# Five columns of a row vector on 128 partitions: turned on chip by DVE and PE instead of gathered from DRAM

## The chip, the cores and the metric

One of the eight cores of a Trainium2 chip runs the whole program. The metric is the time of one execution in device microseconds (us). A profiled execution adds a trace: each instruction of the engines PE (matrix products), PEld (their weight loads), DVE (vector), ACT (scalar functions), POOL and SP (which here only issues DMAs), and each packet that the 16 DMA engines moved.

## What is computed

One token with D = 1024 goes through a layernorm and then through two branches whose results are added to it.

```python
xn = _layernorm(x, axis=-1)
return x + _A_ref(xn, A_k_cache, A_v_cache, A_wq, A_wo) + _B_ref(xn, B_w1, B_w2, B_w3, B_w4)
```

Branch A is attention of 32 query heads on 4 key heads with a cache of 65536 keys of 128 numbers each, in bf16. Branch B mixes through w1 and w2, and adds a feed-forward part; only this part is touched here:

```python
x1 = x + hs
h2 = _gelu(_layernorm(x1, axis=-1) @ w3) @ w4
```

As Sq is 1, the shifted mix is taken apart in the kernel so that w3 needs only the normed token. `h = gelu(xn2 @ w3)` has F = 3584 numbers, and w4 has 3584 rows of 1024.

## The kernel before, in words

**Weights and cache are streamed.** 170 MB come from DRAM through three SBUF slots of 64 KB on each of 128 partitions (`big`, line 71). The list `slots` (lines 117 to 128) sets the order: wq; then for each of the 4 key heads two K pieces and two V pieces in turn (K0, V0, K1, V1 and so on; 8 MB each, and each worked off in two halves of 16384 keys); w3 stands between V0 and K1; w1, the first piece of w4 and the "x4" rows stand after the third head; wo, w2 and the rest of w4 come last. The loop at lines 548 to 555 works off slot i after it has issued slot i + 2 (`ensure`, line 193), and `issue` (line 160) puts one DMA in SP's queue. SP takes its DMAs strictly in this order, and each waits until the slot that it overwrites has been read by its last instruction. So V1 waits for V0's last product, and K2, the next in SP's queue, waits behind V1.

**K** (`compute_K`, line 426): DVE transposes the 8 MB in place, 4 instructions for each half (line 435); PE forms scores (line 439); DVE, PE and ACT form the maximum, the exponential and its transpose `pT` (lines 443 to 476). **V** (`compute_V`, line 479): 32 products add into `oacc`, one PSUM tile with one buffer (line 482). The first half of a head is copied to `og` by ACT (line 491), and each other half is added by DVE (line 494). A half's products wait until `oacc` has been read.

**w3** (`compute_w3`, line 375): 64 products (line 322) give h in rows: h lies on partitions 0, 32, 64 and 96, in two banks of 448 columns each. ACT applies gelu into `hrow` (line 379).

**The bounce** (`bounce`, line 360): w4 needs h on partitions, so POOL writes h to a DRAM scratch `scr_h` (line 363) and reads 3200 of its numbers back as `dst_h`, 25 columns on 128 partitions (line 367). The remaining 384 rows of w4 are the x4 rows: gathered by two indirect DMAs from lines 164 to 171, 70 partitions with 4 rows each and 104 partitions with 1 row each, as the table `XP` (line 24) says. The matching 384 numbers of h are gathered from `scr_h` into columns 25 to 29 of `dst_h` by two more indirect DMAs (lines 369 to 372, issued at line 156): 8 bytes on each of 70 partitions, then 2 bytes on each of 104. A partition without a row has an index out of bounds and keeps the zero that a memset of POOL put there (line 366). The columns are used at line 424, some 190 us later.

**Order of instructions.** The text above gives only the order in which the program is written. A scheduler orders each engine's instructions when the program is built, and pools decide about buffers: `pT` has two (line 76), `pm` in PSUM two (line 80).

Of the kernel before, what the change touches and what calls it, by code (L numbers as in the profile page):

```python
# [8 lines left out]
BF16 = mybir.dt.bfloat16  # L9
F32 = mybir.dt.float32  # L10
# [13 lines left out]
XR = (4, 1)  # L24
XP = (((0, 15), (16, 20), (28, 44), (48, 52), (60, 70), (72, 74), (76, 78), (80, 82), (84, 87), (92, 100), (124, 128)),
      ((0, 20), (28, 52), (60, 88), (92, 120), (124, 128)))
# [5 lines left out]
def kernel(  # L32
# [14 lines left out]
    nc = tc.nc  # L47
    P = 128
# [7 lines left out]
    F = B_w3.shape[1]  # L56
    DC = D // P
    FC = F // P
    NOUT = A_wo.shape[1]
# [4 lines left out]
    FW = F // 8  # L64
# [7 lines left out]
    const = ctx.enter_context(tc.tile_pool(name="const", bufs=1))  # L72
# [3 lines left out]
    tpool = ctx.enter_context(tc.tile_pool(name="tp", bufs=2))  # L76
# [3 lines left out]
    ps_M = ctx.enter_context(tc.tile_pool(name="psM", bufs=2, space=bass.MemoryType.PSUM))  # L80
# [5 lines left out]
    FB = sum(W4_PIECES)  # L86
    w4_v = B_w4[0:P * FB, :].rearrange("(m c) n -> m c n", c=FB)
    x_n = [sum(b - a for a, b in r) for r in XP]
    x_start = [P * FB + sum(XR[j] * x_n[j] for j in range(i)) for i in range(len(XR) + 1)]
    assert x_start[-1] == F and all(x_start[i] % r == 0 and F % r == 0 for i, r in enumerate(XR))  # L90
    wo_v = A_wo.rearrange("(p j) n -> p (j n)", p=P)
    w1_v = B_w1.rearrange("(p c) n -> p (c n)", c=DC)
    w2_v = B_w2.rearrange("(m c) n -> m (c n)", c=DC)
# [4 lines left out]
    def source(piece):  # L98
        kind = piece[0]
        if kind == "wq":  # L100
            return wq_v
        if kind == "w3":
            return w3_v
        if kind == "w1":
            return w1_v
        if kind == "w2":
            return w2_v
        if kind == "wo":
            return wo_v
        if kind == "w4":  # L110
            c0 = w4_start[piece[1]]
            return w4_v[:, c0:c0 + W4_PIECES[piece[1]], :].rearrange("p c n -> p (c n)")
        _, g, t, _ = piece
        cache = A_k_cache if kind == "K" else A_v_cache
        return cache[0, g, t * BK:(t + 1) * BK, :].rearrange("(p k) d -> p (k d)", p=P)
# [14 lines left out]
    st = {}  # L130
# [3 lines left out]
    x_row = []  # L134
# [17 lines left out]
                end = b  # L152
            nc.vector.tensor_copy(out=x_row[i][:], in_=row)

    def gather_rows(i, dst, src):
        nc.gpsimd.indirect_dma_start(out=dst, out_offset=None, in_=src,
                                     in_offset=bass.IndirectOffsetOnAxis(ap=x_row[i][:, 0:1], axis=0),
                                     bounds_check=x_start[i + 1] // XR[i] - 1, oob_is_err=False)

    def issue(pieces):  # L160
        t = big.tile([P, SLOT], BF16, name="slot")
        at = 0
        for piece in pieces:
            if piece[0] == "x4":
                w = sum(XR) * NOUT
                loaded[piece] = t[:, at:at + w]
                nc.gpsimd.memset(loaded[piece], 0.0)  # L167
                for i, r in enumerate(XR):
                    gather_rows(i, t[:, at:at + r * NOUT], B_w4.rearrange("(u r) n -> u (r n)", r=r))
                    at += r * NOUT  # L170
                continue
            src = source(piece)
            w = src.shape[-1]
            nc.sync.dma_start(out=t[:, at:at + w], in_=src)
            loaded[piece] = t[:, at:at + w]
            if piece[0] in ("K", "V"):
                for h in range(HALVES):
                    loaded[(piece[0], piece[1], HALVES * piece[2] + h)] = t[:, h * KEYS:(h + 1) * KEYS]
            at += w
        assert at <= SLOT  # L180
# [3 lines left out]
    for a in range(4):  # L184
        nc.scalar.dma_start(out=x_bf[32 * a:32 * a + 32, :],  # L185
                            in_=A_x[0, 0, 32 * a * DC:(32 * a + 32) * DC].rearrange("(p c) -> p c", c=DC))
# [6 lines left out]
    def ensure(upto):  # L193
        while n_issued[0] <= min(upto, len(slots) - 1):
            issue(slots[n_issued[0]])
            n_issued[0] += 1
# [5 lines left out]
    ident_bf = early[:, 0:64].bitcast(BF16)  # L202
# [68 lines left out]
    for j in range(4):  # L271
# [22 lines left out]
                          in_=sel8[:].unsqueeze(2).to_broadcast([P, 8, 4]))  # L294
# [10 lines left out]
    for b in range(2):  # L305
        for par in range(2):
            nc.vector.tensor_copy(out=psel[:, 2 * b + par, :].rearrange("p (a i) -> p a i", a=4),
                                  in_=iv[:, b, par, :].unsqueeze(1).to_broadcast([P, 4, 32]))


    def rows_product(key, part, wt, xp, width, n_chunks):
        if part == 0:
            st[key] = ps_S.tile([P, 2, 512], F32, name="rows", tag="sc")
        acc = st[key]
        n_c = wt.shape[1]
        for cl in range(n_c):
            c = n_c * part + cl
            for j in range(4):
                for bk in range(2):
                    ch = 4 * bk + j  # L320
                    if ch < n_chunks:
                        nc.tensor.matmul(acc[32 * j:32 * j + 32, bk, 0:width], lhsT=xp[:, c, :],  # L322
                                         rhs=wt[:, cl, ch * width:(ch + 1) * width],
                                         start=(c == 0), stop=(c == DC - 1), tile_position=(0, 32 * j),
                                         skip_group_check=True)
        return acc
# [30 lines left out]
                             skip_group_check=True)  # L357
        nc.vector.tensor_copy(out=qsel[:], in_=pq[:])

    def bounce(rows_ap, view, n, C, tag, extra=False):  # L360
        scr = dram.tile([1, n], BF16, name=f"scr_{tag}")
        flat = scr[0, :]
        nc.gpsimd.dma_start(out=view(flat), in_=rows_ap)
        dst = const.tile([P, C + (sum(XR) if extra else 0)], BF16, name=f"dst_{tag}")
        if extra:
            nc.gpsimd.memset(dst[:, C:], 0.0)
        nc.gpsimd.dma_start(out=dst[:, 0:C], in_=flat[0:P * C].rearrange("(p c) -> p c", c=C))
        if extra:
            at = C
            for i, r in enumerate(XR):  # L370
                gather_rows(i, dst[:, at:at + r], flat.rearrange("(u r) -> u r", r=r))
                at += r
        return dst

    def compute_w3():
        wt = loaded[("w3",)].rearrange("p (c n) -> p c n", n=F)
        acc = rows_product("psh", 0, wt, xpad2, FW, 8)
        hrow = ppool.tile([P, 2, FW], BF16, name="hrow", tag="p")
        nc.scalar.activation(out=hrow[:], in_=acc[:, :, 0:FW], func=ACTF.Gelu_apprx_tanh)
        st["hT"] = bounce(hrow[:].rearrange("(j u) b n -> j u b n", u=32)[:, 0],  # L380
                          lambda f: f.rearrange("(b j n) -> j b n", b=2, j=4), F, FB, "h", True)

    def compute_w1():
        wt = loaded[("w1",)].rearrange("p (c n) -> p c n", n=D)
        acc = rows_product("psh1", 0, wt, xpad2, 512, 2)
        h1row = ppool.tile([64, 512], BF16, name="h1row", tag="p")
        nc.scalar.activation(out=h1row[:], in_=acc[0:64, 0, :], func=ACTF.Gelu_apprx_tanh)
        grow = tpool.tile([64, 512], BF16, name="grow", tag="pT")
        nc.vector.memset(grow[:], 0.0)
        cq = D // 4  # L390
        for grp, shift in enumerate((1, -1, 2, -2)):
            for s in range(S):
                if 0 <= s - shift < S:
                    r0, c0 = 32 * (grp // 2), cq * (grp % 2)
                    nc.vector.tensor_copy(out=grow[r0:r0 + 1, c0:c0 + cq], in_=h1row[r0:r0 + 1, c0:c0 + cq])
        st["gT"] = bounce(grow[:].rearrange("(j u) n -> j u n", u=32)[:, 0],
                          lambda f: f.rearrange("(j n) -> j n", j=2), D, DC, "g")
# [142 lines left out]
    def compute_wo():  # L540
        wt = loaded[("wo",)].rearrange("p (j n) -> p j n", n=NOUT)
        pair_open(wt.shape[1] + DC)
        for j in range(wt.shape[1]):
            pair_acc(oT[:, j:j + 1], wt[:, j, :])

    compute = {"wq": compute_wq, "w3": compute_w3, "w1": compute_w1, "w2": compute_w2, "w4": compute_w4, "x4": compute_x4,
               "wo": compute_wo, "K": compute_K, "V": compute_V}
    for i, pieces in enumerate(slots):
# [37 lines left out]
```

## Time and profile before

| what | value |
|---|---|
| time, median of 3 runs | 403.15 us (402.7 to 404.05) |
| the profiled execution's own time | 402.7 us |
| its span in the profile | 400.9 us |
| mean granted TensorE clock | 0.816 |
| busy: PE, DVE, ACT, POOL | 215.5, 220.8, 35.7, 14.7 us |
| DMA packets and bytes | 4236, 170.11 MB |
| bytes read by the queue of SP's DMAs | 169.09 MB |
| bytes through the queue of POOL's DMAs | 0.81 MB |

Three views matter here. The page divides the span into 40 slices of 10.0 us, with the mean busy share of the 16 DMA engines and what they moved in GB/s in each. The timeline lists instructions by their start, with their length, engine, source line, what they write and read, and in brackets the idle time before them with what ended it. The trace's packet records give start, length and size of each DMA packet. The engines that moved them are not named, but a packet starts within some 10 ns of the end of the one before on its engine, so each engine can be followed from packet to packet.

### The profile page before, as it was taken

What the parts mean: (1) busy time and instruction counts of PE and PEld (TensorE: products, weight loads), DVE (VectorE), ACT (ScalarE), POOL (GpSimd) and SP (SyncE); (2) the same over time, 40 slices, a digit from 0 to 9 for tenths busy, and PEclk for the clock granted to TensorE, in tenths of its full rate; (3) what the DMA queues carried; (4) which work ended last, traced back from release to release, by engine and by line L of the source; (5) the groups of instructions that cost most, each with busy time, mean ns of one, the idle gap of its engine ahead of it and who ended that gap; (6) DMA issues with size and microseconds to landing.
All of it is one profiled execution on the core that took longest, in us unless ns stands there. A gap on an engine that the chain in (4) does not pass through costs nothing.

```text
span 400.9 us, 3470 instructions
## 1 busy us (share of the span) xinstructions
PE 215.5 (54%) x1450; PEld 87.9 (22%) x1450; DVE 220.8 (55%) x319; ACT 35.7 (9%) x62; POOL 14.7 (4%) x24
## 2 busy tenths in 40 slices
PE   0004778630885197409674953395800965295663
PEld 0002223210332032103221321142400422041321
DVE  0007599401986498429846972597503973497300
ACT  0001000500012001100110011001300021001100
POOL 3000000002000000000000004100000000000000
PEclk9999969875698689957955999589865898599757
DMA  9999999999999999999999999999999999999995
GB/s 386 451 419 419 418 420 452 463 427 426 373 446 432 432 426 414 451 432 451 420 438 418 427 458 432 423 427 410 471 419 418 445 438 459 432 419 418 420 416 226
DMA packets 4236, 170.11 MB, mean 424 GB/s; under 512 B 887, under 2 KB 899, under 8 KB 1207
## 3 DMA queue, kind: packets, MB, share of 16 engines
q1 hardware_dynamic: 3608, 169.09, 97.8%
q0 software_dynamic: 416, 0.81, 0.5%
q8 instruction: 11, 0.18, 0.2%
q10 hardware_dynamic: 196, 0.00, 0.0%
q14 instruction: 5, 0.03, 0.0%
HBM read 170.41 MB, written 0.01 MB: 425 GB/s over the span
## 4 chain that ended last, share of the span: by engine, by line
DMA 54%; DVE 32%; PE 10%; another core or an unknown queue 2%; ACT 1%; ACTq 1%; issue 1%; SPq 0%; DVEq 0%
DMA slot<-in_A_k_cache_dram 38%; DVE slot L435 27%; DMA x_row_bf<-in_A_x_dram 9%; DMA slot<-in_B_w_dram 7%; PE oacc L486 4%; PE sc L439 3%; DVE mx L443 3%; PE rows L322 1%; DVE pT L476 1%; PE psB L231 1%; DVE og L494 1%; ACTq L185 0%; PE pm_mx L452 0%; DVE qst L335 0%
## 5 line engine op out<-in xcount | busy, mean ns | idle before, releaser
L439 PE MATMUL sc<-slot,qst 128*128 128x512 bf16 x512 | 136.0, 419 | 100.7 <-DVE slot L435 100.6
L435 DVE STREAM_TRANSPOSE slot<-slot 128x2048 f32<-128x2048 f32 x64 | 142.9, 2280 | 66.4 <-DMA slot<-in_A_k_cache_dram 66.4
L439 PEld LDWEIGHTS <-qst 128*128 128x128 bf16 x512 | 52.1, 104 | 173.0 <-DMA slot<-in_A_k_cache_dram 60.8
L486 PE MATMUL oacc<-slot,pT 128*32 128x512 bf16 x512 | 40.4, 472 | 6.8 <-DVE og L494 3.4
L462 ACT ACTIVATE p_sb<-sc,nm 128x1024 bf16<-128x1024 f32 x16 | 17.8, 1113 | 185.0 <-DVE nm L459 120.7
L476 DVE STREAM_TRANSPOSE pT<-p_sb 128x1024 bf16<-128x1024 bf16 x16 | 19.9, 1244 | 17.3 <-ACT p_sb L462 17.3
L443 DVE TENSOR_REDUCE mx<-sc 128x1 f32<-128x1024 f32 x16 | 19.2, 1203 | 4.5 <-PE sc L439 4.4
L486 PEld LDWEIGHTS <-pT 128*32 128x32 bf16 x512 | 15.4, 112 | 24.9 <-issue 14.0
L494 DVE SCALAR_TENSOR_TENSOR og<-og,alpha,oacc 128x512 f32<-128x512 f32 x12 | 8.8, 735 | 21.6 <-PE oacc L486 21.6
L243 PE MATMUL pm_ln<-early 128*128 128x1 f32 x4 | 1.1, 354 | 33.2 <-DVE early L279 30.6
L237 DVE CAST early<-x_bf 128x8 f32<-128x8 bf16 x1 | 0.2, 172 | 29.0 <-DMA x_bf<-in_A_x_dram 29.0
L445 PE MATMUL pm_mx<-ident_f,mx 128*1 128x128 f32 x16 | 4.3, 270 | 15.9 <-DVE mx L443 15.9
L462 ACT ACT_TABLE_LOAD x3 | 3.8, 1283 | 92.6 <-DVE nm L457 58.0
L167 POOL MEMSET slot<- 128x5120 bf16 x1 | 4.4, 4364 | 148.8 <-PE oacc L486 148.8
L509 PE MATMUL pm_e<-og,sel8q 128*32 128x128 f32 x32 | 6.0, 348 | 5.0 <-DVE og L501 5.0
L243 PEld LDWEIGHTS pm_ln<-early 128*128 128x128 f32 x4 | 1.0, 311 | 33.2 <-issue 30.6
L452 PE MATMUL pm_mx<-ident_f,rep 1*128 1x1 f32 x16 | 3.6, 226 | 8.1 <-DVE rep L449 8.1
L530 PE MATMUL pm_w<-slot,oT 128*1 128x512 bf16 x64 | 6.0, 557 | 3.3 <-DMA slot<-in_A_wo_dram 3.3
L452 PEld LDWEIGHTS pm_mx<-ident_f,rep 1*128 1x128 f32 x16 | 2.3, 142 | 18.2 <-DVE rep L449 18.2
L445 PEld LDWEIGHTS pm_mx<-ident_f,mx 128*1 128x1 f32 x16 | 1.3, 79 | 21.2 <-DVE mx L443 20.4
L509 PEld LDWEIGHTS pm_e<-og,sel8q 128*32 128x32 f32 x32 | 4.1, 139 | 8.3 <-DVE og L501 7.8
L322 PE MATMUL rows<-slot,xpad 128*32 128x448 bf16 (+1 forms) x80 | 5.5, 358 | 0.0
(101 smaller groups left out, 100.1 us busy)
## 6 DMA issues: line engine op xcount, KB each, us to landing
slot<-in_B_w_dram SPq DMA_DIRECT2D x1, 7168.0 KB, 33.0
slot<-in_B_w_dram SPq DMA_DIRECT2D x2, 2048.0 KB, 28.4
slot<-in_B_w_dram SPq DMA_DIRECT2D x1, 3072.0 KB
slot<-in_B_w_dram SPq DMA_DIRECT2D x1, 2304.0 KB, 27.1
slot<-in_B_w_dram SPq DMA_DIRECT2D x1, 768.0 KB
slot<-in_B_w_dram SPq DMA_DIRECT2D x1, 256.0 KB
slot<-in_A_k_cache_dram SPq DMA_DIRECT2D x8, 48.6
slot<-in_A_v_cache_dram SPq DMA_DIRECT2D x8, 37.3
```

Of the source, the lines that this page charges most:

```text
L322: nc.tensor.matmul(acc[32 * j:32 * j + 32, bk, 0:width], lhsT=xp[:, c, :], rhs=wt[:, cl, ch * width:(ch + 1) * width], start=(c == 0), sto ...
L435: nc.vector.transpose(out=kf[:, cg, :], in_=kf[:, cg, :])
L439: nc.tensor.matmul(sc[:, hf, :], lhsT=qst[:, o:o + 128], rhs=kr[:, cg, hf, :, bp // 2, :, bp % 2], start=(cg == 0 and bp == 0), stop=(cg = ...
L443: nc.vector.reduce_max(out=mx[:], in_=sc[:].rearrange("p h n -> p (h n)"), axis=AX.X)
L445: nc.tensor.transpose(pm[0:1, 0:P], mx[:, 0:1], ident_f[:])
L452: nc.tensor.transpose(pm[:, P:P + 1], rep[0:1, :], ident_f[0:1, 0:1])
L462: nc.scalar.activation(out=p_sb[:], in_=sc[:], func=ACTF.Exp, bias=nm[:, 0:1], scale=SCALE, accum_out=lb[:, 0:1])
L476: nc.vector.transpose(out=pT[:], in_=p_sb[:])
L486: nc.tensor.matmul(oacc[32 * u:32 * (u + 1), :], lhsT=pT[:, hf, 32 * t:32 * (t + 1)], rhs=vt[:, :, hf, t, :], start=(hf == 0 and t < 4), s ...
L494: nc.vector.scalar_tensor_tensor(out=st["og"][:], in0=st["og"][:], scalar=alpha[:, 0:1], in1=oacc[:], op0=ALU.mult, op1=ALU.add)
L509: nc.tensor.matmul(pe[rows, 0:P], lhsT=sel8q[:], rhs=og[:, 128 * cg:128 * (cg + 1)], start=(cg == 0), stop=(cg == 3), tile_position=(0, 32 ...
L530: nc.tensor.matmul(psW[32 * q:32 * q + 1, :], lhsT=lhsT, rhs=wrow[:, 512 * b:512 * b + 512], start=(i < 2), stop=(i >= n - 2), tile_positi ...
```

## The change

The two gathers of h and the memset before them go. Instead, compute_w3 takes the 384 numbers from `hrow` where they lie, on partition 96 in the second bank. DVE clears one row of a tile `hx` (5 x 128 numbers on partition 96, in the pool of `pT`) and lays the numbers out in it with 16 small copies, one for each range in `XP`: 11 with 2 to 16 groups of 4 numbers, 5 with 4 to 28 numbers. PE multiplies each of the five rows of 128 with a single 1, which puts it on 128 partitions as a column in PSUM (`pm_hx`), and DVE copies the five columns to `dst_h`. The gathers of the x4 rows of w4 stay, as does the bounce of the 25 other columns.

As built, the order of the two programs differs around this place. On PE, the 64 products of w3 and the five of hx now stand ahead of the second half of V0; before, both halves of V0 stood ahead of w3. On ACT, gelu now stands ahead of the copy of V0's first half to `og`. On DVE, after the second half of K0: the memset, the 16 copies, V0's addition to `og` (line 494), the copy to `dst_h`, and then K1's transposes. The copy to `dst_h` waits for the DMA `dst_h<-scr_h`, which writes the other columns of the same tile. The order of SP's DMAs is the same.

```diff
-    def gather_rows(i, dst, src):
-        nc.gpsimd.indirect_dma_start(out=dst, out_offset=None, in_=src,
-                                     in_offset=bass.IndirectOffsetOnAxis(ap=x_row[i][:, 0:1], axis=0),
-                                     bounds_check=x_start[i + 1] // XR[i] - 1, oob_is_err=False)
...
-        if extra:
-            nc.gpsimd.memset(dst[:, C:], 0.0)
         nc.gpsimd.dma_start(out=dst[:, 0:C], in_=flat[0:P * C].rearrange("(p c) -> p c", c=C))
-        if extra:
-            at = C
-            for i, r in enumerate(XR):
-                gather_rows(i, dst[:, at:at + r], flat.rearrange("(u r) -> u r", r=r))
-                at += r
         return dst
...
+        n_x, last = sum(XR), slice(96, 97)
+        hx = tpool.tile([P, n_x, P], BF16, name="hx", tag="pT")
+        nc.vector.memset(hx[last], 0.0)
+        first = 0
+        for i, r in enumerate(XR):
+            at = x_start[i] - (F - FW)
+            for a, b in XP[i]:
+                nc.vector.tensor_copy(out=hx[last, first:first + r, a:b].rearrange("q r p -> q p r"),
+                                      in_=hrow[last, 1, at:at + r * (b - a)].rearrange("q (p r) -> q p r", r=r))
+                at += r * (b - a)
+            first += r
+        ph = ps_M.tile([P, 512], F32, name="pm_hx", tag="pm")
+        for r in range(n_x):
+            nc.tensor.matmul(ph[:, r:r + 1], lhsT=hx[last, r, :], rhs=ident_bf[last, 96:97], start=(r == 0),
+                             stop=(r == n_x - 1), tile_position=(96, 0), skip_group_check=True)
+        nc.vector.tensor_copy(out=st["hT"][:, FB:FB + n_x], in_=ph[:, 0:n_x])
```

More of the change, by code (lines that the diff above doesn't have):

```diff
@@ L89 @@
     x_start = [P * FB + sum(XR[j] * x_n[j] for j in range(i)) for i in range(len(XR) + 1)]
-    assert x_start[-1] == F and all(x_start[i] % r == 0 and F % r == 0 for i, r in enumerate(XR))
+    assert x_start[-1] == F and x_start[0] >= F - FW and all(x_start[i] % r == 0 and F % r == 0 for i, r in enumerate(XR))
     wo_v = A_wo.rearrange("(p j) n -> p (j n)", p=P)
@@ L168, in issue @@
                 for i, r in enumerate(XR):
-                    gather_rows(i, t[:, at:at + r * NOUT], B_w4.rearrange("(u r) n -> u (r n)", r=r))
+                    nc.gpsimd.indirect_dma_start(out=t[:, at:at + r * NOUT], out_offset=None,
+                                                 in_=B_w4.rearrange("(u r) n -> u (r n)", r=r),
+                                                 in_offset=bass.IndirectOffsetOnAxis(ap=x_row[i][:, 0:1], axis=0),
+                                                 bounds_check=x_start[i + 1] // r - 1, oob_is_err=False)
                     at += r * NOUT
@@ L358, in compute_wq, with bounce @@
         nc.vector.tensor_copy(out=qsel[:], in_=pq[:])
-    def bounce(rows_ap, view, n, C, tag, extra=False):
+    def bounce(rows_ap, view, n, C, tag, extra=0):
         scr = dram.tile([1, n], BF16, name=f"scr_{tag}")
@@ L363, in bounce @@
         nc.gpsimd.dma_start(out=view(flat), in_=rows_ap)
-        dst = const.tile([P, C + (sum(XR) if extra else 0)], BF16, name=f"dst_{tag}")
-        if extra:
-            nc.gpsimd.memset(dst[:, C:], 0.0)
+        dst = const.tile([P, C + extra], BF16, name=f"dst_{tag}")
         nc.gpsimd.dma_start(out=dst[:, 0:C], in_=flat[0:P * C].rearrange("(p c) -> p c", c=C))
-        if extra:
-            at = C
-            for i, r in enumerate(XR):
-                gather_rows(i, dst[:, at:at + r], flat.rearrange("(u r) -> u r", r=r))
-                at += r
         return dst
@@ L380, in compute_w3 @@
         st["hT"] = bounce(hrow[:].rearrange("(j u) b n -> j u b n", u=32)[:, 0],
-                          lambda f: f.rearrange("(b j n) -> j b n", b=2, j=4), F, FB, "h", True)
+                          lambda f: f.rearrange("(b j n) -> j b n", b=2, j=4), F, FB, "h", sum(XR))
+        n_x, last = sum(XR), slice(96, 97)
[14 more added lines that the diff above has]
+        nc.vector.tensor_copy(out=st["hT"][:, FB:FB + n_x], in_=ph[:, 0:n_x])
     def compute_w1():
```

## The prediction, as it was put on record

> **What bounds the kernel.** I read the slices of the page first, then its queues, then the timeline around w3, and last the packet records.
>
> ```profile
> span 400.9 us, 3470 instructions
> ...
> DMA  9999999999999999999999999999999999999995
> GB/s 386 451 419 419 418 420 452 463 427 426 373 446 432 432 426 414 451 432 451 420 438 418 427 458 432 423 427 410 471 419 418 445 438 459 432 419 418 420 416 226
> ...
> q1 hardware_dynamic: 3608, 169.09, 97.8%
> q0 software_dynamic: 416, 0.81, 0.5%
> ```
>
> All 16 DMA engines are busy from the first slice to the last but one, and SP's stream (q1) is 97.8% of the span. No compute engine is over 55%. So the end is set by when the last byte of the stream lands, plus a tail that the change does not touch. An edit counts only if it gives DMA engines time back, or lets them run dry. The eleventh slice, 373 GB/s, is the lowest but the last; that is where the gathers run.
>
> Laid end to end, the packet records from 3 to 395 us show all 16 engines busy except in one place, 109.2 to 110.6 us. There nine engines stand still for 0.65, 0.76, 0.95, 1.00, 1.21, 1.22, 1.23, 1.27 and 1.29 us: 9.6 us, or 0.60 us averaged over 16. Each of the nine starts again with a 16-byte packet of POOL's queue, that is, 8 gathered numbers of 2 bytes: the second gather. The first one's packets (32 to 64 bytes, most near 104 us) show no standstill. The stretches around it, of DVE's transposes with the DMA share and GB/s as the last columns:
>
> ```profile
> 60.00:80.00 20.00, 15.43 (x109) 6.36 (x111) 13.93 (x15) 5.74 (x8) 0.00 (x0) 0.91 1.03 446
> 80.00:100.00 20.00, 3.46 (x72) 1.91 (x65) 1.56 (x2) 0.92 (x1) 3.45 (x4) 0.65 1.02 441
> 100.00:120.00 20.00, 16.74 (x66) 6.74 (x65) 18.43 (x12) 0.99 (x1) 0.00 (x0) 0.84 0.93 394
> 120.00:140.00 20.00, 7.20 (x78) 3.17 (x76) 9.73 (x20) 3.06 (x7) 0.00 (x0) 0.76 1.03 446
> ```
>
> 100 to 120 us has the low share, 0.93. (A packet counts where it starts, so a neighbour can be over 1; the 0.60 us comes from the records.)
>
> **Part 1: the gathers go.** Their own packets are short: between 101.6 and 113.2 us the 29 data packets at 15 ns and the semaphore packets at 9 ns make 0.78 us, 0.05 us over 16 engines. The standstill is the larger term. What it is worth depends on which engine ends last, as each keeps its own partitions of the stream and a delay stays with it. Followed to their ends, the engines finish between 395.98 and 397.16 us. The three last (397.12, 397.15, 397.16) are ones that stood still, for 0.76, 1.29 and 0.95 us; the fourth, at 397.02, did not. By that the end moves only 0.15 us. But among the 2 KB packets of the last microsecond I lose some engines (a chain holds none or 16 of them where each must have 8). So the bounds are 0, if an engine with no standstill is last, and 1.29. I take the mean, 0.60 us, between them; with the packets it is 0.65.
>
> The Trainium skill, "DMA: Bandwidth & Descriptors", section "Queues, rings and completion order", says that each engine takes its queues in turn, a packet at a time. By that rule a gather costs its own packets and no more, 0.05 us, and the time would be 402.65, the second case below. The trace shows the turns (one 64 KB packet of 2.42 us lies between packets of POOL's queue) but also the nine standstills, so I go by the records.
>
> **Part 2: DVE, PE and the slots.**
>
> ```profile
> 74.64 2.65 PE L486 MATMUL oacc<-slot,pT 128*32 128x512 bf16 x32
> ...
> 78.03 2.40 PE L486 MATMUL oacc<-slot,pT 128*32 128x512 bf16 x32 [0.73 <-ACT og L491]
> ...
> 80.25 3.21 PE L322 MATMUL rows<-slot,xpad 128*32 128x448 bf16 x64
> 80.47 0.33 SPq L174 DMA_DIRECT2D slot<-in_A_v_cache_dram  x1
> 80.55 0.75 DVE L494 SCALAR_TENSOR_TENSOR og<-og,alpha,oacc 128x512 f32<-128x512 f32 x1 [2.97 <-PE oacc L486]
> 83.52 0.33 SPq L174 DMA_DIRECT2D slot<-in_A_k_cache_dram  x1
> 83.53 0.92 ACT L379 ACTIVATE hrow<-rows 128x896 bf16<-128x896 f32 x1 [4.25 <-PE rows L322]
> 84.76 0.76 POOL L363 DMA_DIRECT2D scr_h<-hrow  x1 [80.51 <-ACT hrow L379]
> 93.89 0.58 POOL L367 DMA_DIRECT2D dst_h<-scr_h  x1 [8.37 <-DMA scr_h<-hrow]
> 94.78 1.07 POOL L156 DMA_INDIRECT dst_h<-scr_h,x_row  x1 [0.31 <-issue]
> 96.16 1.03 POOL L156 DMA_INDIRECT dst_h<-scr_h,x_row  x1 [0.30 <-issue]
> 99.19 13.28 DVE L435 STREAM_TRANSPOSE slot<-slot 128x2048 f32<-128x2048 f32 x6 [17.89 <-DMA slot<-in_A_k_cache_dram]
> ```
>
> V0's two halves run at 74.64 and 78.03, w3's products at 80.25. SP issues V1 when V0's second half is done (80.47) and K2 when w3's products are done (83.52). DVE has nothing from 81.3 to 99.19, and POOL nothing after 97.2. So the gathers' 2.1 us on POOL cost nothing, and their going saves nothing there.
>
> In the new order w3's products run first. w3 is issued at 46.80 and takes 33.0 us to land: 79.8. Then 3.21 to 83.0, gelu 0.92 to 84.0. No row is a copy of a few numbers on one partition: below stands 0.146 us (line 149, one number on 128 partitions), above 0.395 (line 273, 256 numbers on one partition); nearest is the copy of 128 numbers on 32 partitions, 0.184 us (line 335). So 16 x 0.18 = 2.9 us to 86.9 (2.3 to 6.3). The memset runs before w3 lands. The five products of hx are like line 452 (one row to 128 partitions, 0.226 us with a load of 0.142): at most 1.8 us, at least 0.4; I take 1.2, to 88.1. V0's second half, which waits behind them, 2.40 to 90.5. V1 is issued at 90.5 instead of 80.5, and K2 right behind it.
>
> Is that late? By the records, V1's first packet moved at 96.71, when the first engine was through with K1. The lead shrinks from 16.2 us to 6.2. K1 itself was issued at 71.63 and its first packet moved at 77.33, a lead of 5.7, with no gap. So I cost this at nothing; what hides it is K1's own transfer. At the upper ends (6.3 and 1.8 us) V1 goes at 94.5, still 2.2 us ahead, and a DMA needs some 1.0 us from issue to first packet (wq: 0.75 to 1.78).
>
> DVE's copy to `dst_h` is the added wait. Before, `dst_h<-scr_h` was issued at 93.89 and took 8.6 us to land: 102.5; gelu is now 0.4 us earlier, so about 102.1. Behind the waiting copy stands K1's first transpose, ready at 99.19: it starts at 102.3, 3.1 us late, and so PE's scores, K1's release and V2's issue (120.41 to 123.5). V2's first packet moved at 136.37, so 12.9 us are left. DVE gets the lateness back before K2:
>
> ```profile
> 138.40 4.50 DVE L435 STREAM_TRANSPOSE slot<-slot 128x2048 f32<-128x2048 f32 x2 [4.78 <-DMA slot<-in_A_k_cache_dram]
> ```
>
> 4.78 us idle against 3.1 late: nothing is left of it. The extra instructions come to 3.4 us on DVE and 1.2 on PE, all there. The page's tail after the last byte is the same.
>
> **Sum.** The profiled execution took 402.7 us (span 400.9 and 1.8 around it). 402.7 - 0.60 - 0.05 = 402.05, say **402.1**. It is the lowest of the three runs; their median is 0.45 us higher, so against it the forecast is 1.05 us, or 0.26%, and the range takes that in.
>
> **Rivals.**
> - *The forecast*: feed intact, part of the standstill comes back: 401.6 to 402.4.
> - *An engine with no standstill sets the end*, or the standstill moves to the next small transfer of POOL's queue: then 0.15 us or nothing comes back, 402.5 to 402.7. For: the fourth engine at 397.02. That the change doesn't do what it says to the DMA engines belongs here. Against: bounce writes and reads of the same queue (packets of 400 and 1792 bytes) show no standstill before.
> - *All of it comes back*: the end engine had stood 1.29 us and those at 396.8 to 397.0 were confused with it, or other executions stand still for longer (402.7 to 404.05 is a spread of 1.35 us): 402.7 - 1.29 = 401.4. For: three of the four last engines. Against: seven engines stood not at all.
> - *The stream runs dry at V1*, the case on the slower side. V1 and K2 wait behind hx. It decides when V1 is issued after 95.7 us (96.71 less 1.0), 5.2 us later than I reckon, that is with copies of 0.5 us each. At 0.69 us each (line 501, 512 numbers) hx would cost 8.2 us more: V1 at 98.7, first bytes at 99.7 against 96.7 to 98.7, when the engines come free: 2.0 us dry on the mean, 3.0 on the first: 402.05 + 2.5 = 404.6. Against: no row of so few numbers is above 0.395.
>
> On this last rival the Trainium skill, "SBUF — State Buffer", section "Who interferes with whom", has a rule against the change: DVE copies in a two-port mode lock POOL out of SBUF, so that POOL's DMAs start late. Here POOL would write `scr_h` (0.76 us) among the 16 copies; by the rule the bounce slips at most by their 2.9 us, K1's transposes start at 105, and V2 still has 10 us: the sum stays 402.05. No run here shows POOL's DMA beside such copies.
>
> **Chances.** Forecast 0.50, no return 0.14, all of it 0.20, dry 0.16. About 0.3% (1.2 us) is what a measurement of this kernel can tell from no change. From the median, 401.95 is the edge of "faster": the third case and 0.15 of the forecast's lie below it, so faster 0.35; the dry case is slower, 0.16; same 0.49. The range leaves out most of the dry case and little else: 401.2 to 403.8 (the lower bound is 401.4 less what other runs add, the upper is 402.7 with the 0.45 of the median and the first 0.6 us of a dry stream).
>
> **What would show it.** Right: no low slice between 100 and 120 us; V1 issued near 90.5 and its packets behind K1's without a gap; copies near 0.18 us; K1's transposes near 102.3; V2 near 123.5; K2's start near 138. Wrong: engines idle near 97 to 99 us; a standstill elsewhere; or last packets at 397.1 as before, though no engine stood still.

## The result, and the profile after

The changed kernel takes 402.29 us (median of 11 runs, 402.19 to 403.01), the one before 403.38 (11 runs beside it, 402.70 to 404.58). The ratio is 0.9972, with a 95% interval of 0.9961 to 0.9982: 0.28% faster, 0.18 to 0.39%. The scatter shrank as well, from 1.9 us to 0.8. The profiled execution took 402.19 us. First its page:

```profile
span 400.4 us, 3490 instructions
...
DMA  9999999999999999999999999999999999999995
GB/s 399 439 419 420 419 421 453 451 441 420 426 426 427 420 445 460 419 426 440 432 419 445 447 419 426 447 412 411 450 427 445 452 432 434 426 419 440 445 390 208
...
q1 hardware_dynamic: 3608, 169.09, 97.8%
q0 software_dynamic: 352, 0.80, 0.5%
```

SP's stream is the same 3608 packets, POOL's queue has 64 fewer. The eleventh slice is at 426 GB/s, where it was at 373. The same from the table of stretches, whose last columns are DMA share and GB/s:

```profile
80.00:100.00 20.00, 6.64 (x101) 3.23 (x94) 2.18 (x17) 1.50 (x2) 1.35 (x2) 0.76 1.01 437
100.00:120.00 20.00, 12.12 (x44) 4.83 (x44) 14.55 (x9) 0.00 (x0) 0.00 (x0) 0.67 0.99 426
```

From 100 to 120 us the share went from 0.93 to 0.99. In the packet records no engine stands still between 3 and 395 us. The last weights land at 396.65 us instead of 397.16: 0.51 us, the whole difference of the two profiled executions (402.70 and 402.19). Now the timeline around w3 (products of hx at line 388, V0 at 495, gelu at 370, the copy to `dst_h` at 390):

```profile
79.62 4.69 PE L320 MATMUL rows<-slot,xpad 128*32 128x448 bf16 x64 [2.55 <-DMA slot<-in_B_w_dram]
...
84.38 0.33 SPq L172 DMA_DIRECT2D slot<-in_A_v_cache_dram  x1
84.39 0.92 ACT L370 ACTIVATE hrow<-rows 128x896 bf16<-128x896 f32 x1 [5.57 <-PE rows L320]
85.33 1.44 DVE L382 COPY hx<-hrow 1x60 bf16<-1x60 bf16 x16 [7.34 <-ACT hrow L370]
85.61 0.76 POOL L361 DMA_DIRECT2D scr_h<-hrow  x1 [81.41 <-ACT hrow L370]
...
86.50 0.50 PE L388 MATMUL pm_hx<-early,hx 1*128 1x1 bf16 x5 [2.19 <-DVE hx L382]
...
87.73 1.91 PE L495 MATMUL oacc<-slot,pT 128*32 128x512 bf16 x32 [0.73 <-ACT og L500]
...
89.68 0.33 SPq L172 DMA_DIRECT2D slot<-in_A_k_cache_dram  x1
...
95.41 0.58 POOL L363 DMA_DIRECT2D dst_h<-scr_h  x1 [9.03 <-DMA scr_h<-hrow]
...
105.45 0.17 DVE L390 CAST dst_h<-pm_hx 128x5 bf16<-128x5 f32 x1 [14.95 <-DMA dst_h<-scr_h]
105.53 2.30 DVE L444 STREAM_TRANSPOSE slot<-slot 128x2048 f32<-128x2048 f32 x1
```

The new path takes under 2 us from the end of gelu to the last product of hx, and DVE then stands 15 us at the copy to `dst_h`, with K1 behind it. Nothing of this reaches the stream. Two questions were left for runs: is it the gathers, or the new order of w3, V0 and K1, and what about a gather of so few bytes can cost 1 us?

### The profile page after: what moved, and what is told of

The parts are those of the page before. It is cut to its first block, busy times and chain, and to the rows that moved or that the text cites. A ratio compares the mean times of both kernels' runs of the same rounds, so it can differ in the third digit from the quotient of the medians.

```text
span 400.4 us, 3490 instructions
## 1 busy us (share of the span) xinstructions
PE 224.9 (56%) x1455; PEld 90.8 (23%) x1455; DVE 222.9 (56%) x337; ACT 35.7 (9%) x62; POOL 12.6 (3%) x21
## 3 DMA queue, kind: packets, MB, share of 16 engines
q1 hardware_dynamic: 3608, 169.09, 97.8%
## 4 chain that ended last, share of the span: by engine, by line
DMA 58%; DVE 27%; PE 10%; another core or an unknown queue 2%; ACT 1%; ACTq 1%; issue 1%; SPq 0%; DVEq 0%
DMA slot<-in_A_k_cache_dram 29%; DVE slot L444 22%; DMA slot<-in_B_w_dram 15%; DMA x_row_bf<-in_A_x_dram 9%; PE oacc L495 4%; PE rows L320 3%; DMA dst_h<-scr_h 3%; DMA scr_h<-hrow 2%; DVE mx L452 2%; PE sc L448 2%; DVE pT L485 1%; DVE og L503 1%; ACTq L183 0%; PE psB L229 0%
## 5 line engine op out<-in xcount | busy, mean ns | idle before, releaser
L495 PE MATMUL oacc<-slot,pT 128*32 128x512 bf16 x512 | 46.7, 529 | 5.8 <-DVE og L503 3.0
L495 PEld LDWEIGHTS <-pT 128*32 128x32 bf16 x512 | 17.1, 121 | 26.6 <-issue 21.2
L320 PE MATMUL rows<-slot,xpad 128*32 128x448 bf16 (+1 forms) x80 | 7.4, 463 | 2.5 <-DMA slot<-in_B_w_dram 2.5
L518 PE MATMUL pm_e<-og,sel8q 128*32 128x128 f32 x32 | 5.1, 312 | 4.7 <-DVE og L510 4.7
```

The costliest lines, as they stand in the source:

```text
L495: nc.tensor.matmul(oacc[32 * u:32 * (u + 1), :], lhsT=pT[:, hf, 32 * t:32 * (t + 1)], rhs=vt[:, :, hf, t, :], start=(hf == 0 and t < 4), s ...
L518: nc.tensor.matmul(pe[rows, 0:P], lhsT=sel8q[:], rhs=og[:, 128 * cg:128 * (cg + 1)], start=(cg == 0), stop=(cg == 3), tile_position=(0, 32 ...
```

## The experiments

Each ran on one chip together with the kernel before, and its ratio is to those runs. In the first four the order of all other instructions is that of the kernel they start from.

**Without gathers** (from the kernel before):

```diff
         if extra:
-            at = C
-            for i, r in enumerate(XR):
-                gather_rows(i, dst[:, at:at + r], flat.rearrange("(u r) -> u r", r=r))
-                at += r
```

> Before, with the two gathers of h left out and nothing in their place (the five columns stay zero, so the x4 rows add nothing): the order of all other instructions is that of before. Theory 1, the gathers' standstill is the whole difference: no standstill in the packet records, 402.2 to 402.6 us, as the changed kernel. Theory 2, the new order of w3, V0 and the columns made the difference: 403.1 to 403.6, as before.

402.28 us (9 runs), ratio 0.9973 (0.9961 to 0.9984), no standstill. That is the changed kernel's ratio without its new order. Theory 2 falls.

**The changed kernel with the gathers beside it:**

```diff
+        if extra:
+            spare = const.tile([P, extra], BF16, name="spare")
+            at = 0
+            for i, r in enumerate(XR):
+                nc.gpsimd.indirect_dma_start(out=spare[:, at:at + r], out_offset=None,
...
```

> The changed kernel, with the two gathers put back beside the new path; they write a spare tile that nobody reads. Theory 1: engines stand still again behind the 2-byte gather, about 10 engine-us, and the time is 402.9 to 403.6. Theory 2: 402.2 to 402.6, with or without a standstill.

404.36 us (12 runs, 402.92 to 404.74), ratio 1.0014 (1.0005 to 1.0023): the gain is gone, and the median is above the range that I gave; why this kernel ends even above the kernel before is not shown. The profiled execution, the shortest of the twelve, has 13.5 us of standstill (summed over engines) from 111.5 to 113.5 us. In the table of stretches of this kernel:

```profile
100.00:110.00 10.00, 2.46 (x6) 0.85 (x6) 4.90 (x4) 0.00 (x0) 0.00 (x0) 0.50 1.00 427
110.00:120.00 10.00, 9.71 (x43) 4.02 (x42) 10.00 (x6) 0.00 (x0) 0.00 (x0) 0.95 0.86 360
```

The gathers went out 2.2 us later than in the kernel before (97.01 and 98.39 us), and the hole, share 0.86, moved with them.

**One gather of the two** (the loop's call under `if i == 1`, and under `if i == 0`):

> Before, without the 8-byte gather (its four columns stay zero), the 2-byte gather stays. Theory 1a, the 2-byte elements make the standstill: it is there, some 10 engine-us, 403.0 to 403.6 us. Theory 1b, it takes two gathers one behind the other: none or little, 402.2 to 402.7.

403.60 us (12 runs, 402.71 to 404.88), ratio 1.0004 (0.9989 to 1.0020). The whole cost is there, though the one profiled execution, again the shortest, has only 0.8 us of standstill.

> Before, without the 2-byte gather (its column stays zero), the 8-byte gather stays. Theory 1a: no standstill, 402.2 to 402.7 us. Theory 1b: none as well. If any gather brings a standstill: some 10 engine-us and 403.0 to 403.6.

402.37 us (10 runs, 402.08 to 402.76), ratio 0.9970 (0.9961 to 0.9980), no standstill. So it is the 2-byte gather alone. But is it the 2 bytes? The next three change its size and its rows.

**8 bytes twice**, and the same with 2 bytes for the second (same 70 rows, same index tile):

```diff
+            spare = const.tile([P, 4], BF16, name="spare")
+            for to in (dst[:, C:C + 4], spare[:]):
+                gather_rows(0, to, flat.rearrange("(u r) -> u r", r=XR[0]))
```

> Before, with the second gather replaced by a repetition of the first, 70 rows of 8 bytes, into a spare tile (column 29 stays zero). Theory 1a, 2-byte elements stop the engines: no standstill, 402.2 to 402.7 us. Theory 1c, any second gather close behind another does: a standstill and 403.2 to 404.

403.25 us (12 runs, 402.48 to 404.57), ratio 0.9988 (0.9977 to 0.9999); 3.4 us of standstill at 109 us. Theory 1a expected none.

> As the run with 8 bytes twice (same rows per engine, same index tile, same place in the queue), but the second gather takes 2 bytes for each of the 70 rows. Theory 1a: standstill of some 1 to 13 engine-us in the records, median 403 to 404 us, and a wider spread than without. Theory 1c: the same as with 8 bytes twice. Theory 1d, it takes the 104 rows: none, 402.2 to 402.7.

402.61 us (8 runs, 402.50 to 403.16), ratio 0.9973 (0.9962 to 0.9984); 0.8 us of standstill. No more than with 8 bytes: theory 1a, which expected 403 to 404, fails again. Theory 1c has the first of the pair on its side and not the second; theory 1d has the second and not the first. The 70 numbers lie within 140 neighbouring bytes of the scratch, and by the sizes of the packets the same 13 engines read them that read the 104 rows: seven engines with eight rows, six with two or three.

**4 bytes on the 104 rows** (a third index tile, rows of two numbers):

> Before, with the second gather taking 4 bytes (two neighbouring numbers) for each of the same 104 partitions, into a spare tile (column 29 stays zero); two small DVE instructions at the start make its index. Theory 1a with the limit between 2 and 4 bytes: no standstill, 402.2 to 402.7 us. Theory 1d, it is the number of rows, or a limit above 4 bytes: a standstill, 403 to 404.

403.51 us (12 runs, 402.21 to 404.75), ratio 0.9992 (0.9978 to 1.0007); 9.5 us of standstill. So 2 and 4 bytes cost alike, and theory 1a, that 2-byte elements stop the engines, is dropped. The 104 rows matter, or what they read: 13 of the 16 engines, with eight rows each, all from 208 or 416 neighbouring bytes of the scratch.

**Where the rows lie.** In place of the two gathers of h, one gather of 2 bytes on the same 104 partitions that reads w4, issued at 77 us, once spread and once close (`step` times 1024 or times 1 in two copies of one kernel):

```diff
+        nc.vector.tensor_scalar(out=step, in0=row, scalar1=1024.0, scalar2=None, op0=ALU.mult)
+        nc.vector.tensor_copy(out=x_row2[:], in_=step)
...
+            spare = tpool.tile([P, 1], BF16, name="spare", tag="pT")
+            nc.gpsimd.indirect_dma_start(out=spare[:], out_offset=None, in_=B_w4.rearrange("f (u r) -> (f u) r", r=1),
+                                         in_offset=bass.IndirectOffsetOnAxis(ap=x_row2[:, 0:1], axis=0),
+                                         bounds_check=1024 * F - 1, oob_is_err=False)
```

> Before without the gathers of h; in their place one gather of 2 bytes for the same 104 partitions that does not touch the scratch: from w4, each 2 KB apart from the next, into a spare tile, issued once the first half of V0 has freed a buffer (the five columns stay zero). Theory 2a, reads by many engines at once of a few hundred neighbouring bytes stop them: no standstill, 402.2 to 402.7 us. Theory 2b, 104 valid rows of a gather do, wherever they lie: a standstill and 403 to 404.

402.64 us (12 runs, 402.10 to 403.18), ratio 0.9967 (0.9953 to 0.9980), no standstill.

> The same as with the spread rows, but the 104 numbers of w4 lie next to each other (208 bytes). Theory 2a: a standstill of 1 to 13 engine-us, 403 to 404 us. Theory 2b: the same as with the spread rows. Theory 2c, the bytes must have been written just before, as in the scratch: none, 402.2 to 402.7.

404.00 us (12 runs, 403.49 to 404.86), ratio 1.0005 (0.9989 to 1.0021); 13.8 us of standstill between 82.0 and 85.0 us. The two kernels differ in one multiplier, and in both the records show 13 packets of 16 bytes. Here is the slice that holds the gather's packets, the ninth, first spread:

```profile
GB/s 386 451 419 420 419 420 446 463 434 419 419 432 427 425 478 427 419 419 445 420 445 458 420 419 425 450 441 388 445 465 425 445 432 414 419 438 471 433 374 184
```

and close:

```profile
GB/s 372 463 418 419 417 419 451 475 335 444 437 444 439 424 412 445 437 431 450 426 417 444 432 437 444 434 415 396 455 444 424 457 450 413 418 431 444 434 400 187
```

434 against 335 GB/s. Theory 2b falls, as 104 rows far apart bring no standstill; 2c falls, as bytes that nobody had just written bring one. Of 2a it is shown that the 104 rows must lie close. That closeness is enough is not shown: the 70 numbers within 140 bytes, read by the same 13 engines, cost only 0.8 us. That the engines read at the same time was not varied.

**The columns in their own tile** (from the changed kernel):

```diff
-        nc.vector.tensor_copy(out=st["hT"][:, FB:FB + n_x], in_=ph[:, 0:n_x])
+        st["hX"] = const.tile([P, n_x], BF16, name="hX")
+        nc.vector.tensor_copy(out=st["hX"][:], in_=ph[:, 0:n_x])
```

> The changed kernel, with the five columns in a tile of their own, so that DVE's copy no longer waits for the bounce. If the wait costs nothing, as reckoned: 402.2 to 402.5 us as the changed kernel, with the first transposes of K1 back at 99.0 to 99.3 instead of 105.5. If the late K1 costs time at the end: 0.3 us or more below the changed kernel.

```profile
85.57 0.17 DVE L391 CAST hX<-pm_hx 128x5 bf16<-128x5 f32 x1 [0.27 <-PE pm_hx L388]
...
99.00 8.89 DVE L445 STREAM_TRANSPOSE slot<-slot 128x2048 f32<-128x2048 f32 x4 [9.96 <-DMA slot<-in_A_k_cache_dram]
```

K1 starts at 99.00 us, as K1 lands. The time is 402.44 us (6 runs, 402.11 to 402.52), ratio 0.9964 (0.9951 to 0.9978), which overlaps the changed kernel's. DVE's wait of 15 us costs nothing that can be measured.

**Rows moved between engines** (from the kernel with its own tile; only `XP` differs: partitions 62, 63, 94 and 95 out, 70, 74, 78 and 82 in):

> The changed kernel with the columns in a tile of their own, and two of the 4-row partitions taken from each of two DMA engines (the one of partitions 28 to 31 and 60 to 63, and the one of 92 to 95 and 124 to 127) and given to four engines that had two such partitions (70, 74, 78, 82). In the records without a standstill one or two engines with a full load of x4 rows end at 396.4 to 396.7 us, the others before 396.2. If these two are the late ones: 401.8 to 402.1 us, last data near 396.2. If others are: 402.2 to 402.5, no change.

402.65 us (12 runs, 402.11 to 403.30), ratio 0.9974 (0.9959 to 0.9989); last data at 396.59 us, 396.56 without the move. A miss: two engines still end at 396.20 and 396.59, and the other 14 before 395.8, so the late ones are others than I took them for. By these ends at most 0.8 us, an estimate, lies there for whoever finds them. The Trainium skill ("DMA: Bandwidth & Descriptors", section "Latency and other measured facts") says that engines 7 and 15 are usually the slower ones; by that page's layout ("The descriptor swizzle") these are the two that I unloaded. Here unloading them left the last data where it was, 396.59 against 396.56 us. As the records name no engine, that is all that is shown.

**The kernel before, once more:**

> The kernel before, for a second profile. If the standstill behind the second gather makes the scatter of its times: there again, of another size, and the span differs from 400.9 us as the end of its last engine does.

403.91 us, and this is what the scatter looks like. Fewer engine-us are lost than in the first profile (5.6 against 9.6; 0.3 of them behind the first gather), but one engine stands 2.30 us. Followed by its packets to 150 us it is 1.8 us behind the next, and at the end one engine lands 1.1 us after all others. The last products of the two profiles before and of the one after, in this order:

```profile
396.91 1.02 PE L231 MATMUL psB<-slot,dst_h 128*1 128x256 bf16 x16 [0.66 <-DMA slot<-in_B_w_dram]
```

```profile
398.25 0.89 PE L231 MATMUL psB<-slot,dst_h 128*1 128x256 bf16 x16 [0.66 <-DMA slot<-in_B_w_dram]
```

```profile
396.39 1.01 PE L229 MATMUL psB<-slot,dst_h 128*1 128x256 bf16 x16 [0.71 <-DMA slot<-in_B_w_dram]
```

Each waits for the last piece of w4. All profiles together, with the standstill from the packet records (3 to 394.5 us, summed over engines):

| kernel | gather(s) of h | its time, us | standstill, us | last data, us |
|---|---|---|---|---|
| before | 8 B x 70, 2 B x 104 | 402.70 | 9.6 | 397.16 |
| before, once more | the same | 403.91 | 5.6 | 398.49 |
| after | none | 402.19 | 0 | 396.65 |
| without gathers | none | 402.30 | 0 | 396.64 |
| after, with gathers | both | 402.92 | 13.5 | 397.50 |
| one gather | 2 B x 104 | 402.71 | 0.8 | 397.15 |
| one gather | 8 B x 70 | 402.17 | 0 | 396.61 |
| 8 bytes twice | 8 B x 70, twice | 402.83 | 3.4 | 397.32 |
| 2 bytes, 70 rows | 8 B x 70, 2 B x 70 | 402.64 | 0.8 | 396.97 |
| 4 bytes | 8 B x 70, 4 B x 104 | 403.23 | 9.5 | 397.74 |
| own tile | none | 402.11 | 0.1 | 396.56 |
| rows moved | none | 402.11 | 0 | 396.59 |
| spread, from w4 | 2 B x 104 | 402.63 | 0 | 397.05 |
| close, from w4 | 2 B x 104 | 403.65 | 13.8 | 398.09 |

The time follows the last column, 5.4 to 5.7 us above it in every row, and not the sum of the standstills: one engine that is late is enough. The rows without a standstill end at 396.6 but for one at 397.05, whose lateness I can't explain. In the row of the 2-byte gather alone, too, the end is 0.5 us late though no engine stood longer than 0.4 us.

## Why the prediction was right, and where it was not

**What bounds the kernel**: right. 0.51 us of earlier data is 0.51 us of time between the two profiled executions.

**Part 1, the size.** The forecast from the profiled execution was 402.1, measured 402.19 for the profiled one and 402.29 for the median. I took the mean of the standstills, 0.60 us, and not the 0.15 that following single engines to their ends gave; 0.51 came. The mean came close by luck: the time goes by the last engine, and the table shows that sum and end don't go together. From median to median it is 1.09 us, against 1.05 in the forecast. That fits what I had put into the third rival, that other executions stand still for longer. The second profile of the kernel before shows one, 403.91 us with 2.30 us on one engine. The standstill and the scatter of the times go together: with the 2-byte or 4-byte gather on 104 rows the runs of a kernel spread over 1.4 to 2.8 us, without gathers over 0.4 to 1.2. The 1.2 us are those of the kernel with the rows moved, so a part of the scatter has another source. The gathers' own packets between 101.6 and 113.2 us, which I summed to 0.78 us, come to 0.83 with all semaphore packets; over 16 engines that is 0.05 us either way.

**The cause.** I had put the standstill on the second gather, which holds, and took its mark, eight numbers of 2 bytes, for a reason to expect it of that gather alone. The size is not it (4 bytes cost the same, 2 bytes on 70 rows far less). For the 104 rows it is how close they lie; what the 70 rows lack is open. The prediction's second case, that a gather costs no more than its own packets, gave 402.65. The runs don't bear it out where 104 rows lie close, and do where they are spread. It was drawn from the rule that each engine takes its queues in turn (the Trainium skill, "DMA: Bandwidth & Descriptors", section "Queues, rings and completion order"); the turns are in the trace, but they don't bound what a gather costs.

**Part 2, the steps beside the stream.** The sum charged them nothing, and that held, but four of its steps were off.
- *V1's issue.* I let V1 wait for V0's second half, 90.5 us. V1 went at 84.38, as soon as w3's products were done, and K2 at 89.68. As w3 is now read before V0, V1 got w3's slot and K2 got V0's. I carried over the waits of the kernel before. The lead over V1's first packet, which I had at 6 us, was thus 12.
- *w3's products* took 4.69 us, not 3.21. PE had stood for 2.55 us, and its granted clock was lower, 0.68 against 1.00. Before and after, the clock being the third figure from the end:

```profile
80.25:83.46 3.21, 3.21 (x68) 1.69 (x60) 0.75 (x1) 0.00 (x0) 0.00 (x0) 1.00 0.88 373
```

```profile
79.62:84.31 4.69, 4.69 (x64) 2.13 (x64) 0.00 (x0) 0.00 (x0) 0.00 (x0) 0.68 1.03 447
```

  In the kernel with its own tile the same 64 products, after 2.05 us of waiting, took 3.22 us; in the kernels with the gathers put back and with the rows moved, after 2.87 and 2.68 us, they took 4.91. In these four the longer wait goes with the longer products; what sets the clock is not shown.
- *The copies* took 1.44 us for all 16, not 2.9: each row reads 0.158 to 0.416 us, but they overlap and start 0.09 us apart. The five products took 0.50 us, not 1.2. The rival of a stream that runs dry needed copies of 0.5 us and was far off.
- *The bounce* landed at 105.4, not 102.1. Gelu came 1.3 us later than reckoned, and both DMAs took longer to land:

```profile
scr_h<-hrow POOLq DMA_DIRECT2D x1, 7.0 KB, 9.5
dst_h<-scr_h POOLq DMA_DIRECT2D x1, 6.2 KB, 10.0
```

  So K1's transposes started at 105.53 instead of 102.3, V2 went at 126.73 instead of 123.5, and the 4.78 us of idle DVE before K2 did not quite cover it:

```profile
139.82 2.29 DVE L444 STREAM_TRANSPOSE slot<-slot 128x2048 f32<-128x2048 f32 x1
```

  1.4 us later than before. V3 goes 1.4 us later too (161.03 against 159.62), and from V4 (197.76 against 199.16) the lateness is gone. The DMAs still in SP's queue covered it: V2's first packet moved 8.7 us after its issue.

The Trainium skill's rule that DVE copies in a two-port mode lock POOL out ("SBUF — State Buffer", section "Who interferes with whom") left no mark in the time, and no run shows whether these copies are in that mode: POOL's instruction that issues `scr_h` took 0.76 us among the copies and 0.76 us without them, and its DMA landed after 9.3 to 9.7 us in the four kernels with the copies, after 8.2 to 10.0 us in the others.

**The change's sign.** 0.28% lies just inside the 0.3% that I took for what can be told from no change; the interval, 0.18 to 0.39%, excludes no change.

## What to carry to other kernels

In a kernel whose DMA engines are never idle, lay the packet records end to end and look for places where engines stand: a transfer of a few hundred bytes can stop the stream for longer than its own packets take, and the time goes by the engine that ends last, not by the mean. Before taking small gathers away, look at where their rows lie: at steps of 2 KB the gather of 104 rows cost nothing that could be measured (402.64 us, and 402.65 in a kernel without a gather on the same chip). And when a change alters which buffer is read first, don't carry the waits of the old program over, but read which buffer each load gets in the new one.

## What the runs showed of the hardware

- Reads of 104 numbers of 2 bytes by 13 DMA engines: within 208 bytes the engines stood for 13.8 us in all, at 2 KB steps for 0 (ratios to the same kernel 1.0005 and 0.9967). While an engine stands for such a packet it moves nothing of its other queue either.
- The length of the standstill varies from execution to execution: the kernel before lost 9.6 us over nine engines in one, and 5.6 us with 2.30 us on one engine in another.
- Open: why a first gather of 8 bytes on 70 rows hardly stops an engine (0.3 us in one of seven profiles, nothing in the others), and its repetition 1.4 us later did (3.4 us); why 2 bytes on the 70 rows cost less (0.8 us); and what makes close reads wait. No run here looked into these.
- A POOL transfer of 6 to 7 KB took 8.2 to 10.0 us to land beside the stream in all profiles; on each engine a 64 KB packet of 2.42 us lies between two packets of POOL's queue.
